# RWKV attention followed by a feed-forward block on one core: a new start-up (small loads issued by GpSimd, r of pair 0 behind k, tables from two banks) and a new order

## The chip, the cores and the metric

The kernel runs on one core of one Trainium2 chip. Its engines work beside each other, each through a queue of its own in the order written: TensorE (PE, matmuls), VectorE (DVE), ScalarE (ACT), GpSimd (POOL) and SyncE (SP, which here only issues transfers). They wait for each other through semaphores. The metric is the device time of the whole program in microseconds (us), median of the runs.

## What is computed

The reference, cut to what matters (B = 4, H = 8 heads, S = 768 steps, D = 48; the result of the first part, seen as 4 x 768 x 384, is the input of the second):

```python
state = 0
for t in range(S):                                   # for every batch and head
    cur = outer(u * k[t], v[t])
    y[t] = r[t] @ (state + cur)
    state = w[:, None] * state + outer(k[t], v[t])
# second part, x = y with the heads side by side (C = 384)
mu = mean(x); var = mean((x - mu) ** 2)
xn = (x - mu) / sqrt(var + 1e-6) * g_ln
out = x + maximum(xn @ w_ch1, 0) @ w_ch2             # 384 -> 1536 -> 384
```

## The kernel before, in words

The 4 x 768 steps are 24 tiles of 128 steps, six to a batch. Within a tile the recurrence is done as masked attention: k is multiplied by powers w^-(t+1) and r by powers w^t (the tables Fk and Fr), both are transposed on PE or by a transposing transfer, `AT` multiplies them into scores, `AM` masks them on DVE, `S` makes the tile's state (and the column sums for the u term), `ZU` scales the state with the decay, `Y` adds the state's and the scores' parts, `X` adds the u term. The second part of each tile: `SQ` and `RS` for the norm, `XN` centres, `LT` and `XT` (or `LTD`) transpose, `UP` is the first product (12 matmuls a step), `RL` the relu out of PSUM, `DN` the second product, `OT` the sum, `STO` the store.

The first four tiles are two pairs. A pair is loaded in one transfer for each of k, r and v (`LK2`, `LR2`, `LV2`, 384 KB each), and its steps have a 2 in their names: `SK2` and `SR2` multiply by the tables `Fk2` and `Fr2`, `TRk2` and `TRr2` transpose into PSUM, `TCk2` and `TCr2` copy that to SBUF, `Q2` multiplies the two transposed tensors, `AT2`, `AM2`, `CC2`, `VB2`, `Y2` as above. For pair 0 k is done by halves of the heads (`SKH`, `TRH`).

The tables come from w: `WF` loads w as a row, `LN` takes its logarithm into `ln_row` (whose other rows `MO` sets to 0, and `ones` to 1), `WBM` spreads the row over the 128 partitions with a matmul by ones, and `FK2`, `FR2`, `FK`, `FR` are ACT exponentials of that with a power of each partition (`MI2` makes `pow2` and `MI` makes `pow_i` and the identity on GpSimd). `ROWS` loads w, u and g_ln as 11 rows; `RM` turns them into columns on PE, `RC` copies them out; `UW`, `WL`, `UGC` make from them the u term's factors, the decay of a tile (WLZ) and -g. `SW` folds -g into the first weights (`LW1` loads them), `IW2` loads the second weights with a cast through GpSimd. `MP`, `MZ`, `MM`, `MM2`, `MR` are memsets and masks. `DU,n` is n columns of dummy matmuls on zeros.

All steps stand in one list, PLAN, written out. An entry is step, number and engine (`v` DVE, `s` ACT, `g` GpSimd, `-` the engine that the step always has; for a transfer the letter names the queue: `-` SP, `s` ACT). The entries are issued in this order, so each engine's queue is the list cut to its steps; nothing is moved later. The waits follow from the tiles' users. Buffers are rings (SLOTS; four of `ot`, so OT of tile i + 4 waits for the store of tile i); in PSUM two banks serve `hp`, and `at` (two banks wide), `s`, `y`, `tr` and `o` have one buffer each. In the program's transfers eight semaphores take turns, so that a transfer from SP or ACT waits for the one eight before it.

Lines that matter: L225 and L223 issue the rows, L304 is LN, L314 WBM, L321 the tables, L203 every product of two tensors, L200 and L198 every copy, L299 and L301 the dummies, L532 the pair transposes, L431 and L580 AT, L448 and L590 AM, L461 to L476 S of a pair, L715 UP, L743 DN, L799 OT, L809 the stores.

Of the kernel before, what the change touches and what calls it, by code (L numbers as in the profile page):

```python
# [29 lines left out]
UP,33,- RL,32,s LK,7,- RS,1,s Y,4,- RL,33,s UP,34,- XT,3,s DN,5,- SQ,2,s TRr2,3,- RL,34,s UP,48,- RS,2,s TCr2,3,v SK,5,g DN,6,- LR2,4,- MP,6,g UP,49,-  # L30
OT,1,v VB,4,g LV,6,- TRk,5,- DN,0,- TCk,5,v SK,6,v DN,1,- LK,8,- RL,48,s ZU,4,v TRk,6,- Q,5,v DN,2,- TCk,6,s SK,7,v AT,5,- LK,11,- OT,0,v Q,6,g
UP,50,- X,4,v LK,9,- TRk,7,- AM,5,v SR2,4,g DN,8,- XN,4,s SQ,3,s DN,9,- LV,7,- TCk,7,v CV,5,s S,5,- DN,10,- RL,49,v RL,50,s SK,8,g LR2,5,- LT,4,-
CC,5,s AT,6,- OT,2,v XT,4,s Y,5,- VB,5,g AM,6,v SQ,4,s LK,10,- UP,64,- CV,6,s SK,11,g UP,65,- SK,9,v RL,64,s LR2,6,- TRr2,4,- X,5,v S,6,- TCr2,4,s
DN,12,- Q,7,v TDk,4,- XN,5,g ZU,6,v Y,6,- DN,13,- SR2,5,v CV,7,g RL,65,s LT,5,- LV,8,- RS,3,s AT,7,- SK,10,v DN,14,- XT,5,s RS,4,s UP,66,- CC,6,s
STO,0,- OT,3,v VB,6,g LV,9,- UP,80,- AM,7,v RL,66,s SR2,6,g TRr2,5,- SQ,5,s TDk,5,- S,7,- X,6,v TCr2,5,s DN,16,- ZU,7,v AT,9,- Q,8,v UP,81,- RL,80,s
LK,13,- ZD,7,v CC,7,v AM,9,v Y,7,- VB,7,g TRr2,6,- STO,3,- DN,17,- CV,8,g STO,1,- TCr2,6,s XN,6,v LK,12,- DN,18,- X,7,v UP,82,- STO,2,- CV,9,s OT,4,v
RL,81,s LV,10,- S,8,- Q,10,v AT,8,- RL,82,s ZU,8,v DN,20,- RS,5,s Q,9,v ZD,8,g CC,8,s AM,8,v XN,7,s DN,21,- LK,15,- LT,6,- S,9,- XT,6,s DN,22,-
ZU,9,v SQ,6,s LV,13,- UP,96,- VB,8,v CC,9,v OT,5,v LT,7,- VB,9,g Y,9,- RL,96,s UP,98,- STO,5,- XT,7,s ZD,9,g X,9,v LV,11,- AT,10,- CV,10,v UP,97,-
LK,14,- XN,9,g SK,12,v Y,8,- SK,13,g RL,97,s DN,24,- AM,10,v RL,98,s LV,12,- DN,25,- RS,6,s Q,11,g SQ,7,s X,8,v LT,9,- S,10,- TDk,6,- UP,112,- CC,10,v
XN,8,v VB,10,g DN,26,- RL,112,s LR2,7,- UP,113,- SQ,9,s SK,15,g OT,6,v LK,16,- Y,10,- ZU,10,v RL,113,s UP,114,- XT,9,v ZD,10,g X,10,v LT,8,- AT,11,- RL,114,s  # L40
LV,15,- DN,28,- SK,14,g XT,8,s AM,11,v CV,12,s S,11,- UP,130,- CV,11,g LK,17,- UP,131,- RL,130,v Y,11,- LV,14,- Q,12,v RL,131,s UP,129,- CC,11,s XN,10,s VB,11,g
AT,13,- LR,17,- RL,129,s DN,29,- SR2,7,g CV,13,s X,11,v UP,128,- AM,13,v XN,11,s S,12,- RS,7,s UP,133,- LTD,9,- SQ,8,s ZU,12,v Q,13,g DN,30,- RL,128,v SQ,10,s
TRr2,7,- STO,4,- OT,7,v RL,133,s CV,15,g UP,132,- LR,16,- SQ,11,s SK,17,g AT,12,- TDk,7,- RL,132,v TCr2,7,s DN,32,- CV,14,g SK,16,v DN,33,- LR,19,- CC,12,s RS,8,s
AM,12,v VB,12,g DN,34,- S,13,- LV,16,- SR,17,g UP,149,- OT,8,v CC,13,s UP,147,- VB,13,g RL,149,s LK,19,- Y,13,- RL,147,v SR,16,g DN,36,- X,13,v STO,6,- UP,145,-
Q,14,g ZU,13,v TDr,8,- Y,12,- UP,146,- RL,145,v XN,13,g Q,15,v DN,37,- RL,146,s X,12,v AT,14,- DN,38,- XN,12,s AM,14,v UP,144,- LTD,10,- OT,9,v UP,148,- RL,144,s
ZD,13,v S,14,- RS,9,s TDk,8,- DN,40,- SK,19,v RL,148,s ZU,14,v AT,15,- SQ,12,s Y,14,- LK,18,- AM,15,v CC,14,s DN,41,- VB,14,g STO,7,- S,15,- LR,18,- DN,42,-
X,14,v CV,16,v UP,163,- XN,14,s ZD,14,v LV,18,- UP,165,- OT,10,v RL,163,s Q,16,v Y,15,- RL,165,s ZU,15,v UP,161,- LV,19,- CC,15,s SQ,13,s VB,15,g UP,160,- RL,161,s
LV,17,- AT,17,- X,15,v RS,10,s DN,44,- RL,160,s AM,17,v XN,15,g DN,45,- ZD,15,g CV,18,s LTD,11,- DN,46,- SK,18,v SR,19,g UP,164,- OT,11,v STO,8,- UP,162,- TDk,9,-
RL,164,s Q,17,g AT,16,- RL,162,s DN,48,- AM,16,v LK,21,- SR,18,g DN,49,- S,16,- UP,177,- TDr,9,- CC,16,v ZU,16,v DN,50,- RL,177,s ZD,16,v UP,176,- VB,16,v STO,9,-
OT,12,v LR,20,- Y,16,- RL,176,s S,17,- STO,10,- UP,181,- X,16,v CC,17,s LK,20,- VB,17,g UP,178,- RL,181,s CV,17,g DN,52,- SQ,14,s LR,21,- Q,19,g Y,17,- SQ,15,s  # L50
DN,53,- X,17,v XN,16,s DN,54,- RL,178,s RS,11,s UP,180,- OT,13,v XN,17,s AT,18,- Q,18,v RL,180,s UP,179,- LTD,12,- AM,18,v SK,20,g CV,19,s DN,56,- RL,179,s SK,21,v
LV,20,- S,18,- DN,57,- ZU,18,v CC,18,s STO,11,- SQ,17,s VB,18,g Y,18,- STO,12,- AT,19,- DN,58,- TDk,10,- SR,20,g AM,19,v UP,197,- SR,21,g X,18,v UP,195,- RL,197,s
OT,14,v S,19,- TDr,10,- SQ,16,s UP,193,- RL,195,v CC,19,s CV,20,s Y,19,- ZU,19,v XN,18,s DN,60,- LV,21,- VB,19,v ZD,19,g DN,61,- X,19,v RL,193,v UP,192,- XN,19,s
SQ,19,s DN,62,- LTD,13,- RL,192,v RS,12,s UP,194,- OT,15,v SQ,18,s UP,196,- Q,21,v LV,22,- RL,194,s Q,20,v AT,20,- LR,23,- RL,196,s DN,64,- AM,20,v RS,13,s DN,65,-
CV,21,s LR,22,- S,20,- DN,66,- LK,23,- ZU,20,v UP,211,- ZD,20,g OT,16,v LK,22,- AT,21,- CC,20,v RL,211,s UP,213,- SR,23,g AM,21,v STO,13,- S,21,- UP,208,- STO,14,-
CC,21,s RL,213,s ZU,21,v VB,21,g Y,21,- SR,22,v RL,208,s DN,68,- X,21,v DN,69,- TDr,11,- VB,20,v XN,21,g DN,70,- UP,209,- SK,23,g OT,17,v LTD,15,- Y,20,- SK,22,v
RL,209,s UP,210,- CV,22,s X,20,v TDk,11,- UP,212,- RL,210,s DN,72,- SQ,20,s RL,212,v DN,73,- XN,20,s SQ,21,s DN,74,- LTD,14,- UP,242,- OT,18,v UP,241,- LV,23,- ZD,21,v
# [55 lines left out]

# [738 lines left out]
```

## Time and profile before

| | before |
|---|---|
| median of 3 runs | 148.47 us (148.46 to 148.66) |
| profiled execution | 147.94 us |
| its span, first to last instruction | 146.2 us |
| PE busy | 140.7 us (96%) |
| DVE, ACT, POOL busy | 108.5, 88.7, 76.8 us |
| transfers | 27.24 MB, 186 GB/s over the span |
| dummy columns in PLAN | 12880 |
| first AT2 of pair 0 starts | 10.53 us |
| first UP starts | 20.32 us |

A row of the timeline gives start, duration, engine, line, operation, the tiles by name (buffer numbers left out), the number of instructions merged, and in brackets the idle time before with what ended it. `SPq`, `ACTq`, `POOLq` are the issuing of a transfer; the transfer itself goes on after that. A tile's name is that of its buffer: `sc<-kf,Fk` is SK or SKH, `sc<-rf,Fr` is SR, `trs<-tr` is TC, `A<-at,mask` is AM. In a stretch table the columns are the stretch, the sum of busy time (with number of instructions) of PE, weight loads, DVE, ACT and POOL, the granted clock of PE, the share of the transfer engines, and GB/s.

### The profile page before, as it was taken

Reading aid. Unit: us, or ns where it says so; the run is one execution under the profiler, and the core shown is the slowest. Engines: PE = TensorE matmul, PEld = TensorE weight load, DVE = VectorE, ACT = ScalarE, POOL = GpSimd, SP = SyncE. Lnnn points to the kernel's source line nnn. Section 1 sums busy time; section 2 is a strip of 40 time slices with the busy share of each in tenths; the row PEclk is TensorE's granted clock in tenths of the full one; section 3 lists DMA queues with packets and bytes.
Section 4 is the critical chain, followed back from the end, with each engine's and each line's share of the span. In section 5 each row is a group of like instructions: output and inputs, shape, how many; then the busy total and the mean of one; then the engine's idle time right before and its main releaser. Section 6 shows DMA issues by size and latency. Waiting matters only on the chain.

```text
span 146.2 us, 4682 instructions
## 1 busy us (share of the span) xinstructions
PE 140.7 (96%) x1909; PEld 110.3 (75%) x1909; DVE 108.5 (74%) x207; ACT 88.7 (61%) x211; POOL 76.8 (53%) x107
## 2 busy tenths in 40 slices
PE   6899999999999999999999999999999999998990
...
GB/s 114 246 322 393 350 238 227 212 239 170 248 69 188 96 305 213 193 220 168 166 204 186 126 211 149 215 229 148 222 104 207 262 114 100 108 31 172 106 86 99
DMA packets 86021, 27.24 MB, mean 186 GB/s; under 512 B 81260, under 2 KB 84464, under 8 KB 86000
## 3 DMA queue, kind: packets, MB, share of 16 engines
...
q0 software_dynamic: 432, 1.18, 4.5%
q10 hardware_dynamic: 2086, 0.79, 2.1%
...
q14 instruction: 6, 0.05, 0.1%
HBM read 18.88 MB, written 4.72 MB: 161 GB/s over the span
## 4 chain that ended last, share of the span: by engine, by line
PE 86%; DVE 4%; POOL 3%; DMA 1%; SPq 1%; issue 1%; ACT 1%; POOLq 0%; ACTq 0%; DVEq 0%
PE hp L715 32%; PE o L743 30%; PE at L580 5%; PE y L652 3%; PE tr L532 2%; PE s L615 2%; PE y L644 2%; PE o L299 2%; DVE sc L203 1%; DMA out_dram<-ot 1%; PE y L511 1%; PE tr L700 1%; PE s L602 1%; SPq L809 1%; PE s L476 1%
## 5 line engine op out<-in xcount | busy, mean ns | idle before, releaser
L715 PE MATMUL hp<-xT,w_sb 128*128 128x128 bf16 (+1 forms) x648 | 57.0, 237 | 0.0
L731 ACT ACTIVATE hT<-hp 128x512 bf16<-128x512 f32 x58 | 34.1, 594 | 32.7 <-PE hp L715 29.5
L743 PE MATMUL o<-w_sb,hT 128*128 128x384 bf16 x276 | 52.9, 326 | 0.4 <-DVE ot L799 0.4
L715 PEld LDWEIGHTS <-w_sb 128*128 128x128 bf16 x648 | 49.0, 114 | 3.7 <-DMA xT<-xn 0.2
L743 PEld LDWEIGHTS <-hT 128*128 128x128 bf16 x276 | 24.4, 97 | 13.3 <-issue 0.5
L590 DVE TENSOR_TENSOR A<-at,mask 128x1024 bf16<-128x1024 f32 x20 | 24.4, 1220 | 2.8 <-PE at L580 2.8
L634 POOL TENSOR_TENSOR Vb<-vf,cc 128x384 f32<-128x384 f32 x15 | 13.2, 879 | 20.5 <-ACT cc L198 13.4
L799 DVE SCALAR_TENSOR_TENSOR ot<-o,rs,x 128x384 f32<-128x384 f32 x23 | 14.2, 616 | 9.1 <-PE o L743 5.9
L659 DVE SCALAR_TENSOR_TENSOR x<-y,Vb 128x384 f32<-128x384 f32 x24 | 13.2, 551 | 8.0 <-POOL Vb L634 4.4
L203 POOL TENSOR_TENSOR q<-trs,trs 128x512 bf16<-128x512 bf16 x9 | 10.5, 1170 | 10.5 <-ACT trs L198 5.9
L203 POOL TENSOR_TENSOR sc<-rf,Fr 128x384 bf16<-128x384 f32 (+1 forms) x11 | 14.6, 1331 | 1.7 <-DMA rf<-in_r_dram 1.6
L666 ACT ACTIVATE sqj<-x,sm 128x384 bf16<-128x384 f32 x24 | 14.6, 609 | 0.1
L198 ACT COPY trs<-tr 128x1024 bf16<-128x1024 bf16 (+1 forms) x10 | 10.8, 1075 | 4.0 <-PE tr L532 3.6
L203 DVE TENSOR_TENSOR sc<-kf,Fk 128x384 bf16<-128x384 f32 (+1 forms) x14 | 10.3, 739 | 3.0 <-ACT Fk L321 2.9
L733 DVE TENSOR_SCALAR hT<-hp 128x512 bf16<-128x512 f32 x14 | 9.6, 688 | 3.9 <-PE hp L715 3.8
L203 POOL TENSOR_TENSOR Z<-ZS,WLZ 128x384 bf16<-128x384 f32 x7 | 7.3, 1045 | 9.8 <-DVE ZS L628 9.8
L673 ACT ACTIVATE xn<-x,sm 128x384 bf16<-128x384 f32 x14 | 8.6, 612 | 4.3 <-DVE x L659 4.2
L203 POOL TENSOR_TENSOR sc<-kf,Fk 128x384 bf16<-128x384 f32 x9 | 9.0, 1000 | 3.0 <-DMA kf<-in_k_dram 3.0
L299 PE MATMUL o<-warm 128*128 128x512 bf16 x21 | 7.1, 463 | 1.2 <-DVE warm L250 1.2
L580 PE MATMUL at<-trs,trs 48*128 48x128 bf16 x160 | 7.9, 219 | 0.0
L198 ACT CAST vv<-vf 128x384 bf16<-128x384 f32 (+1 forms) x13 | 6.9, 531 | 1.0 <-DMA vf<-in_v_dram 0.9
L628 DVE TENSOR_TENSOR ZS<-s,Z 128x384 f32<-128x384 f32 x12 | 6.6, 553 | 0.8 <-PE s L615 0.7
...
## 6 DMA issues: line engine op xcount, KB each, us to landing
...
```

Of the source, the lines that this page charges most:

```text
L198: nc.scalar.copy(out=out, in_=in_)
L203: engines[e].tensor_tensor(out=out, in0=in0, in1=in1, op=ALU.mult)
L299: nc.tensor.matmul(out=warm_ps[0][:], lhsT=warm[:, :P], rhs=warm[:], start=True, stop=True)
L580: nc.tensor.matmul(out=t[:, par, q, :], lhsT=kT(i)[p0 : p0 + D, q, :], rhs=rT(i)[p0 : p0 + D, q, :], start=True, stop=True,)
L590: engines[e].tensor_tensor(out=eqt(AA(i)[:]), in0=eqt(src[:]), in1=mask[:].unsqueeze(1).to_broadcast([P, H, P]), op=ALU.mult)
L634: engines[e].tensor_tensor(out=heads(Vb(i)), in0=vf(i), in1=cc(i)[:].unsqueeze(2).to_broadcast([P, H, D]), op=ALU.mult,)
L659: nc.vector.scalar_tensor_tensor(out=xx(i)[:], in0=psum["y", i][:, :C], scalar=1.0, in1=Vb(i), op0=ALU.mult, op1=ALU.add, accum_out=sm[i][:],)
L666: nc.scalar.activation(out=sqj[:], in_=xx(i)[:], func=ACT.Square, bias=sm[i][:], scale=-float(C), accum_out=sq[g][:, j : j + 1])
L715: nc.tensor.matmul(out=t[:, a * gw : (a + 1) * gw], lhsT=w1_sb[n][kc][:, fb::FB], rhs=xT(g)[:, :size, kc, :], start=(kc == 0), stop=(kc == ...
L731: nc.scalar.activation(out=o, in_=s, func=ACT.Relu)
L743: nc.tensor.matmul(out=psum["o", i][:, :C], lhsT=hT(g)[:, fk, j * P : (j + 1) * P], rhs=w2_sb[d][:, a, :], start=(fk == 0), stop=(fk == FK ...
L799: nc.vector.scalar_tensor_tensor(out=ot(i)[:], in0=psum["o", i][:, :C], scalar=rs[g][:, j : j + 1], in1=xx(i)[:], op0=ALU.mult, op1=ALU.add,)
```

## The change

The code adds a queue for GpSimd's transfers and the steps `SRH`, `TRG` and `GQ`; it splits `FK`, `FR` and `FR2` by halves of the heads; and it gives the two halves of WBM two banks (`y` and `hp`) in place of the two banks of `at`. The transposed r of pair 0 goes to an `hp` bank in place of `tr`. The diff, with PLAN cut to its first lines, and then two places near its end:

```diff
-MW,0,v LV2,0,s WF,0,- MZ,0,v MM2,0,g LK2,0,- MO,0,v TL,0,s MP,2,v MR,0,v MP,0,g MI,0,g ROWS,1,- ROWS,0,- MI2,0,g IDF,0,v LN,0,s LR2,0,- MP,7,g ROWS,2,s
-DU,3104,- WBM,0,- MM,0,g LK2,1,- MP,3,g CV2,0,g WBM,1,- FK2,0,s FK2,1,s LR2,1,- FK2,2,s SKH,0,v FK2,3,s DU,1008,- RM,0,- FR2,0,s SKH,1,v DU,176,- TRH,0,- LR2,2,s LV2,1,-
-MP,1,v DU,176,- TRH,1,- MP,5,v FR2,1,s TCk2,0,s SR2,0,v FR,0,s SK2,1,v DU,3008,- TRr2,0,- RC,0,s FK,0,s UW,0,g TCr2,0,v WL,0,s LW1,0,- MP,4,v DU,2304,- AT2,0,-
-Q2,0,v SR2,1,g LW1,1,- AM2,0,v DU,640,- S,0,- LK,4,- TRk2,1,- ZU,0,v AT2,1,- LW1,2,- TCk2,1,s CC2,0,v VB2,0,g AM2,1,v CV2,1,s DU,2048,- TRr2,1,- LV,4,- SR2,2,v
-S,1,- TCr2,1,s Y2,1,- ZU,1,v UGC,0,s Q2,1,v TRr2,2,- SW,0,s SW,2,g AT2,2,- X,1,v S,2,- TCr2,2,s AM2,2,v DU,416,- Y2,0,- LR2,3,- XN,1,s ZU,2,v CC2,1,s
+MW,0,v LK2,0,s WF,0,- MP,0,v MP,3,g MZ,0,v MM2,0,g LR2,0,- TL,0,s MR,0,v MP,2,v MP,1,v MO,0,v ROWS,2,g LK2,1,- LN,0,s MI2,0,g LV2,0,s DU,2592,- WBM,0,-
+ROWS,0,g LR2,1,- WBM,1,- ROWS,1,g FK2,0,s FK2,1,s MI,0,g FR2,1,s SKH,0,v FK2,2,s FK2,3,s IDF,0,g MP,5,v FR2,0,s DU,1648,- TRH,0,- SKH,1,v FR2,2,s LR2,2,- SRH,0,v
+FR2,3,s DU,400,- TRH,1,- RM,0,- SRH,1,v TCk2,0,s SK2,1,v TRG,0,- TRG,1,- LV2,1,- RC,0,s FK,1,s TCr2,0,v UW,0,g UGC,0,s FR,1,s FK,0,s Q2,0,v DU,2256,- AT2,0,-
+LW1,0,- CV2,0,s TRk2,1,- AM2,0,v GQ,0,g WL,0,s LW1,1,- S,0,- SR2,1,g TCk2,1,s LK,4,- ZU,0,v DU,832,- AT2,1,- MP,7,v CC2,0,s LW1,2,- FR,0,s DU,592,- S,1,-
+AM2,1,v SR2,2,g TRr2,1,- ZU,1,v LV,4,- DU,64,- Y2,1,- TCr2,1,s VB2,0,v CV2,1,s DU,688,- TRr2,2,- Q2,1,v AT2,2,- TCr2,2,s X,1,v DU,336,- S,2,- AM2,2,v XN,1,g
+SW,2,s SW,1,g DU,368,- LT,1,- Y2,0,- LR2,3,- SW,0,s CC2,1,v XT,1,v MP,4,v ZU,2,v SW,3,g SW,5,s AT2,3,- SK,4,v UP,16,- IW2,0,g SW,4,s X,0,v TRk,4,-
...
-UP,225,- OT,19,v XN,22,s AT,23,- RS,14,g SQ,22,s UP,226,- LTD,16,- AM,23,v RL,225,s RS,16,g DN,80,- RL,226,s STO,18,- S,23,- Y,23,- CC,23,s STO,16,- DN,81,- VB,23,g
-UP,240,- X,23,v DN,82,- RL,240,s XN,23,g UP,257,- OT,20,v LTD,17,- UP,256,- RL,257,s DN,84,- SQ,23,s RL,256,v STO,17,- UP,258,- STO,20,- RS,17,g DN,85,- RL,258,v RS,15,g
+LTD,15,- Y,20,- SQ,21,s SK,23,v UP,213,- RL,211,s DN,68,- STO,13,- RL,213,v TDk,11,- UP,210,- X,20,v DN,69,- ZU,21,v RL,210,s XN,20,v STO,16,- DN,70,- SQ,20,s LTD,14,-
+UP,225,- LTD,16,- S,23,- UP,242,- OT,19,v CC,23,s RL,225,s Y,23,- VB,23,v RL,242,s DN,80,- X,23,v DN,81,- SQ,23,s DN,82,- XN,23,s RS,17,g UP,257,- OT,20,v LTD,17,-
...
-    queues = {"-": nc.sync, "s": nc.scalar}
+    queues = {"-": nc.sync, "s": nc.scalar, "g": nc.gpsimd}
...
+    told = const.tile([1, 2], BF16, name="told")
...
+    def SRH(h, e):
+        hh = slice(h * HP, (h + 1) * HP)
+        times(e, sc(1)[:, :, hh, :D], slots(rf2(0))[:, :, hh], Fr2[:, :, hh])
+
+    def TRG(h, e):
+        for j in range(2):
+            q0 = j * HP + h * (HP // 2)
+            turn(1, q0, q0 + HP // 2)
+
+    def GQ(i, e):
+        engines[e].tensor_copy(out=told[:], in_=q2[0][0:1, 0, 0, 0:2])
...
     def WBM(i, e):
-        if i == 0:
-            psum["wb"] = ps.tile([P, 2, HP, P], FP32, name="at")
-        half_bank = psum["wb"][:, i].rearrange("p q t -> p (q t)")[:, :CH]
-        nc.tensor.matmul(out=half_bank, lhsT=ones[:], rhs=ln_row[:, i * CH : (i + 1) * CH], start=True, stop=True)
-
-    def table(out, pw, h=None):
-        src = psum["wb"][:].rearrange("p b q t -> p b (q t)")[:, :, :CH]
-        dst = out.rearrange("p (b h) d -> p b (h d)", b=2)
-        if h is not None:
-            src, dst = src[:, h], dst[:, h]
-        nc.scalar.activation(out=dst, in_=src, func=ACT.Exp, scale=pw)
-
-    def FK_(i, e):
-        table(Fk[:], pow_i[:, 1:2])
-
-    def FR_(i, e):
-        table(Fr[:], pow_i[:, 0:1])
-
-    def FR2(j, e):
-        table(Fr2[:, j], pow2[:, j : j + 1])
+        p = psum["wb", i] = (ps_h if i else ps).tile([P, 512], FP32, name="hp" if i else "y")
+        nc.tensor.matmul(out=p[:, :CH], lhsT=ones[:], rhs=ln_row[:, i * CH : (i + 1) * CH], start=True, stop=True)
+
+    def table(out, pw, h):
+        dst = out[:, h * HP : (h + 1) * HP].rearrange("p h d -> p (h d)")
+        nc.scalar.activation(out=dst, in_=psum["wb", h][:, :CH], func=ACT.Exp, scale=pw)
+
+    def FK_(h, e):
+        table(Fk[:], pow_i[:, 1:2], h)
+
+    def FR_(h, e):
+        table(Fr[:], pow_i[:, 0:1], h)
+
+    def FR2(i, e):
+        h, j = divmod(i, 2)
+        table(Fr2[:, j], pow2[:, j : j + 1], h)
...
-            psum["tr", i] = ps.tile([P, 2 * HP, P], BF16, name="tr")
+            psum["tr", i] = ps_h.tile([P, 2 * HP, P], BF16, name="hp") if i == 1 else ps.tile([P, 2 * HP, P], BF16, name="tr")
```

All other lines of PLAN differ too: the same steps in another order and in part on other engines. The dummy columns are 9776 in all, 2592 of them ahead of WBM. For some steps the engine changes: CC of a tile is on DVE 11 times (6 before), SK on GpSimd 13 times (9), SR2 on GpSimd 6 of 7 (4 of 8), RL on DVE 17 of 72 (14).

More of the change, by code (lines that the diff above doesn't have):

```diff
@@ L30 @@
[L30 to L57, printed above, removed]
@@ new lines @@
+XN,3,s Y2,2,- SW,8,v SW,7,g RL,1,v LK,6,- UP,0,- MP,6,g X,2,v IW2,2,g UP,2,- RL,0,s XN,2,v DN,4,- Q,4,g RL,2,s LT,2,- SQ,0,s UP,18,- XT,2,v
+MM,0,g CV,4,v UP,32,- RL,18,v LK,7,- S,4,- RL,32,v LT,3,- UP,34,- XT,3,s AM,4,v UP,33,- RL,34,s DN,5,- SR2,3,v CC,4,s RL,33,s VB,4,g UP,48,- LV,5,-
+TRr2,3,- SK,5,g Y,4,- TCr2,3,s DN,6,- LR2,4,- X,4,v UP,49,- OT,1,v XN,4,g SQ,3,s LV,6,- TRk,5,- SK,6,v DN,0,- TCk,5,s DN,1,- LK,8,- Q,5,v RL,48,s
+ZU,4,v TRk,6,- RS,0,s AT,5,- SK,7,v TCk,6,s DN,2,- LV,8,- RL,49,v SR2,4,g S,5,- LT,4,- OT,0,v UP,50,- CC,5,s LK,9,- XT,4,s AM,5,v RS,3,s DN,8,-
```

37 lines of the change are left out of this document (30 added, 7 removed).

## The prediction

> **What bounds the kernel now.** I read the page's parts 1 and 2 first, then the waits of TensorE, then the timeline of the first 21 us, the stretch table, and the end of the chain.
>
> ```profile
> PE 140.7 (96%) x1909; PEld 110.3 (75%) x1909; DVE 108.5 (74%) x207; ACT 88.7 (61%) x211; POOL 76.8 (53%) x107
> ...
> PE   6899999999999999999999999999999999998990
> ```
>
> TensorE (PE) is busy all along. So the time is three things: when the real work can begin, how many dummy columns (DU) stand in PE's queue, and what stalls the new order brings. The real matmuls are the same before and after.
>
> ```profile
> 1.18 2.74 PE L299 MATMUL o<-warm 128*128 128x512 bf16 x6 [1.18 <-DVE warm L250]
> ...
> 2.40 0.80 SPq L225 DMA_DIRECT2D x<-in_u_dram  x1
> ...
> 2.48 0.52 ACT L304 ACTIVATE ln_row<-x 1x384 f32<-1x384 f32 x1
> ...
> 3.78 1.63 PE L314 MATMUL at<-ln_row,ones 128*128 128x192 f32 x4
> ...
> 3.92 0.44 SPq L394 DMA_DIRECT2D rf<-in_r_dram  x1
> ...
> 5.51 0.42 ACT L321 ACTIVATE Fk<-at,pow 128x192 f32<-128x192 f32 x1 [2.50 <-POOL vv L200]
> ...
> 6.27 1.18 DVE L203 TENSOR_TENSOR sc<-kf,Fk 128x384 bf16<-128x384 f32 x2 [2.91 <-ACT Fk L321]
> ...
> 9.66 0.69 DVE L200 COPY trs<-tr 128x1024 bf16<-128x1024 bf16 x1
> ...
> 10.53 0.42 PE L431 MATMUL at<-trs,trs 48*64 48x128 bf16 x16
> ...
> 20.32 1.53 PE L715 MATMUL hp<-xT,w_sb 128*128 128x128 bf16 x24
> ```
>
> Columns: start, duration, engine, line. The first table (5.51) starts 0.10 after the fourth broadcast matmul ends at 5.41: both halves lie in one tile, so it waits for both. r of pair 0 is issued only at 3.92, behind u and w on SP. The first real score matmul (AT2,0) starts at 10.53, the first UP at 20.32. The dummies end within 0.1 us of what the next real matmul waits for (10.50 against the copy's end at 10.35), so their column counts are close to real waits.
>
> ```profile
> 2.00:4.00 2.00, 2.00 (x7) 0.87 (x6) 0.54 (x4) 0.99 (x2) 1.76 (x12) 1.00 0.99 255
> 4.00:6.00 2.00, 2.00 (x6) 1.19 (x6) 0.00 (x0) 0.49 (x2) 1.44 (x4) 1.00 0.80 183
> 6.00:8.00 2.00, 1.55 (x15) 1.06 (x15) 1.56 (x5) 1.86 (x6) 0.00 (x0) 1.00 1.17 323
> ```
>
> The last column is GB/s: the transfers have a hole at 4 to 6 us, because r was issued late.
>
> ```profile
> 128.59 1.24 DVE A L590
> 129.83 1.41 SPq L809
> 131.30 2.09 DMA out_dram<-ot
> 133.47 0.63 DVE ot L799
> ```
>
> The chain's only late detour: OT,20 waits for the store of tile 16, issued late. PE's idle time there is 0.37. Between 20 us and there I find no PE wait above 0.2 us.
>
> **The start, step by step.** I walk the new order with durations of these rows; "before" times stand in brackets.
>
> *Logarithm and tables.* On DVE the memsets are reordered: four that now stand ahead of ln_row's take 0.13 to 0.20 each, so ln_row ends at 2.65 (2.10) and LN runs 2.70 to 3.22 (3.00). Five 512-column dummies at 0.43 and a short one end PE's lead at 3.34 (3.71), so WBM,0 starts at 3.41 (3.78). Its two matmuls end 0.99 later, 4.40; the other half is in another bank, so the first table starts at 4.50, 1.0 earlier. Tables follow 0.31 apart with 0.42 each: FK2,1 ends 5.23, FK2,3 6.14, FR2,0 6.45, FR2,3 7.06. FR2 in halves adds two ACT instructions, inside this pace.
>
> *Loads.* k takes v's place on ACT's queue at 0.72; v landed in 3.4, so k lands at 4.1. r is second on SP at 1.14, where k was (landed 5.3), so r lands at 5.3. k of pair 1 and v follow without the hole: at 323 GB/s, 384 KB take 1.2, so both are in by 7.6.
>
> *Rows on GpSimd.* Three small loads leave SP (0.80, 0.63) and ACT (0.51) and are put into POOL's queue. POOL's three DMA issues in the trace (L369) cost 0.59 to 0.79 each; an ACT or SP issue is 0.4 to 0.8, a POOL memset 0.31. I take 0.6, bounds 0.3 and 0.8. They also move past the memset of sc and the masks (0.3, 1.3). Behind them on POOL wait pow2 (3.7, needed 4.50) and the identity: 0.72 + 0.3 + 1.4 + 3 x 0.6 + 0.5 + 0.75 = 5.5, bounds 4.6 and 6.1. Its user, TRH,0, needs SKH,0 too (5.26 to 5.82), and PE's dummies end about 6.0 to 6.2. So the issues cost nothing; uncovered, they would cost 0.2 each.
>
> *Pair 0.* SKH,1 runs 6.17 to 6.73, SRH,0 6.65 to 7.21, SRH,1 7.13 to 7.69, SK2,1 7.6 to 8.57 (0.96 at 8.74 before), TCr2,0 to 9.2 (0.69). TRH,1 is done at 7.2, so ACT's copy TCk2,0 (1.01) ends at 8.3. PE: TRH, RM, TRG end at 8.0, 2256 dummies at 216 ns per 512 take 0.95. DVE's copy ends last: AT2,0 at 9.3 (10.53), 1.2 earlier.
>
> *The row columns.* RM now stands in PE's queue between TRH,1 and TRG,0 and waits for all three rows; TRG and everything of PE queue behind it. The last row (u) is issued at about 4.4. Hardware-queue rows took 2.6 to 3.2 from issue (u: 2.40 to 5.63); POOL's 384 KB loads took 5.1 at least. RM is free to wait until 7.6 (then TRG 0.45, its drain 0.2, and DVE is ready at 8.5); later than that, each us costs one. I take 3.0, so 7.4, at no cost, because the size is that of the first row; the other end lands at 9.5 and costs 1.9.
>
> For such a load the Trainium skill ("DMA: Bandwidth & Descriptors", section Anatomy of one DMA) gives about 2.0 us fixed plus bytes over bandwidth. By that u would land near 6.4 and RM would not wait; by the trace's 5.1 it would be 9.5. No small load on that queue is in the trace.
>
> *From there to UP,16.* CV2,0 moves from POOL to ACT (0.83). ACT then carries TCk2,0, five short ones, the cast, WLZ (until 11.1), TCk2,1 (until 12.0), and CC2,0 (until 12.1), for which S,1 waits because it reuses the bank: PE is idle some 0.4 there (11.8 to 12.2). Before, PE had 0.29 idle at 16.6. GQ (0.15, nearest the 0.17 of a small copy) makes POOL wait for Q2,0's end at 9.8; behind it are SR2,1 and SR2,2 at 1.81 each, until 13.6. TRr2,1 is reached at 12.9 and TRr2,2 at 14.5, so GQ costs nothing there. Without it POOL would start SR2,1 when r of pair 1 lands, about 8.8, beside Q2: the trace has the same DVE product at 0.96 alone (7.84) and 1.62 beside a POOL product (14.10), so up to 0.7 on the chain to S,0.
>
> The Trainium skill ("SBUF — State Buffer", section Who interferes with whom) says that a two-input VectorE operation and a reading GpSimd operation exclude each other. That agrees with the 1.62, and puts the guard's worth at the full rest of POOL's product; the sum stays.
>
> AT2,1, TRr2,1, Y2,1, AT2,2, S,2, LT,1, Y2,0, AT2,3 then follow on PE with waits under 0.1, and UP,16 starts at 18.1. Its weight slices end at 17.9 (SW,0 on ACT). S,3 and TRk,4, which stood ahead of it, come after: 0.93. So like for like 19.05 against 20.32: 1.25 earlier. This holds 224 fewer dummy columns after AT2,0 (0.1) and the rest from AT2,0.
>
> **The rest of the list.** STO,16 moves far ahead of OT,20, so the 0.37 wait at 133.5 should go: a gain of 0.4. Against it, in four places two AT steps that share the bank stand 1.83 to 1.95 of PE work apart from start to start (AT,8/10, 18/19, 20/21, 22/23; never under 2.7 before). From an AT's start to its mask's end is 1.61 (128.22 to 129.83). That leaves 0.2 to 0.3 if DVE is free; a DVE operation in the way (0.55 to 0.62) makes 0.3 to 0.4 each. Bounds 0 and 1.5; I take 0.4, as DVE is busy three quarters of the time but planned around. Net zero.
>
> Sum: -1.25 - 0.4 + 0.4 = -1.25. The profiled execution is 147.94 with a span of 146.2; its span should become about 144.95. It lies 0.5 under the median of 148.47, to which I apply the same difference: 147.2.
>
> **Rivals.**
> 1. *The rows land late (slower).* Place: RM in PE's queue. Speaks for it: POOL's loads took 5.1 to 7.2. Against: those are 256 times larger. AT2,0 comes 1.65 after the landing (RM, TRG, dummies). Break-even is a landing at about 8.9; with 5.1 it is 9.5 to 9.6, AT2,0 at 11.2, and with ACT's columns late as well the kernel ends 0.6 slower: 149.1.
> 2. *The early gain is lost in the rest.* DVE late at the four AT pairs and elsewhere for 0.7 more than taken: 147.9 (mild). The store wait kept, 1.5 at the pairs and 0.1 or more elsewhere: 148.8 and above (severe, on the slower side too).
> 3. *The gain is cut* because PE runs at half speed longer. Before 6 us 512 columns take 0.43, later 0.22. If that change came 3 us later, TRH, TRG and 400 dummies would take 1.05 more, 0.3 of it free before DVE's copy ends; AT2,0 would be at 10.05 and the result 148.0. Against: PE has no gap until 6 in either order.
>
> The Trainium skill ("TensorE: Matmul & The Clock Gate", Part 1) states that the full clock comes after one busy window of about 3.4 us. The trace agrees: half pace from 1.18 to about 6, then full. By that rule rival 3 needs the window to end in the thinner stretch after 6.2.
>
> **Chances.** Forecast 0.59, rival 2 mild 0.12, rival 3 0.05; rows late by about 1 us (147.9 to 148.7) 0.07; rival 1 in full 0.08, rival 2 severe 0.09, for an order of 120 us that I did not walk. A measurement of this kernel tells about 0.2% (0.3 us) from no change: faster is under 148.17, slower above 148.77. Faster: 0.59 + 0.12 + 0.05 = 0.76. Same: 0.07. Slower: 0.08 + 0.09 = 0.17. The range: low 146.5 (no AT stalls, and 0.3 more from the walk); high 148.7, which leaves out the slower cases.
>
> **What would show it.** First table at 4.5; r landed by 5.4; AT2,0 near 9.3, ended by DVE's copy; UP,16 near 18.1; no wait of OT on a store near 132. Wrong if RM waits past 7.6, if the identity ends after 6.2, or if PE shows waits on DVE's masks (L599 there) that sum above 1 us.

## The result, and the profile after

The changed kernel takes 150.33 us in the median (148.5 to 155.95, 20 executions), the kernel before 148.27 (147.56 to 150.52, 20 executions beside them). The ratio is 1.0109 (95% interval 1.008 to 1.0137): slower by 1.1%, where 147.2 was forecast. Every ratio in this document leaves out executions more than 1.5% above the quickest of the same kernel (here six, above 150.7), while the medians and ranges hold all. The execution that was profiled is one of the quickest: 148.82, span 147.0, against 147.94 and 146.2 before.

The page of the changed kernel, parts 1 and 2:

```profile
PE 139.9 (95%) x1903; PEld 110.5 (75%) x1905; DVE 110.9 (75%) x217; ACT 87.3 (59%) x202; POOL 84.0 (57%) x115
...
PE   6959999999899999999999999999999999999991
```

PE does 0.8 less work (dummies) and the span is 0.8 longer, so 1.6 more stands idle. The 5 in the third slice (7.35 to 11.0) is new. The timeline of the start, in the manner of the rows before (L325 is WBM, L329 the tables, L541 the pair transposes, L236 RM, L440 AT2, L724 UP):

```profile
3.35 0.99 PE L325 MATMUL y<-ln_row,ones 128*128 128x192 f32 x2
...
4.21 0.60 POOL L226 DMA_DIRECT2D x<-in_u_dram  x1
4.44 0.73 ACT L329 ACTIVATE Fk<-y,pow 128x192 f32<-128x192 f32 x2 [1.23 <-PE y L325]
...
5.30 0.61 POOL L272 TENSOR_SCALAR_AFFINE_SELECT ident<-ident 128x128 bf16<-128x128 bf16 x1
...
6.91 0.54 PE L541 MATMUL tr<-ident,sc 128*128 128x128 bf16 x4
...
9.00 0.36 PE L236 MATMUL s<-idf,x 11*128 11x11 f32 x2 [1.56 <-DMA x<-in_u_dram]
...
10.79 0.42 PE L440 MATMUL at<-trs,trs 48*64 48x128 bf16 x16
...
19.39 0.80 PE L724 MATMUL hp<-xT,w_sb 128*128 128x128 bf16 x11
```

The first table starts at 4.44 (5.51 before). k landed at 4.21, r at 5.41. DVE is done with both products of r at 7.63, and PE with k's transposes at 7.45. But PE stands at RM until 9.00, because u's row, issued at 4.21, lands at 8.87. AT2,0 starts at 10.79, later than the 10.53 before. UP,16 starts at 19.39; with the two steps moved behind it (0.93) that is 20.32, the same as before. The chain of waits has it as one long piece (start, duration, what):

```profile
4.21 4.66 DMA x<-in_u_dram
```

The stretch table of the changed kernel has no hole in the transfers at 4 to 6 us (183 GB/s before), and next to no PE in the 1.8 us ahead of RM:

```profile
4.00:6.00 2.00, 2.00 (x7) 1.06 (x6) 0.70 (x2) 1.56 (x6) 1.80 (x7) 1.00 1.17 324
...
7.20:9.00 1.80, 0.24 (x4) 0.10 (x2) 1.30 (x2) 1.01 (x1) 0.00 (x0) 1.00 1.18 321
```

At the other end the chain is PE alone where it went through a store of tile 16 before:

```profile
131.81 1.97 PE o L752 x12
133.78 0.04 issue
133.82 1.53 PE hp L724 x24
```

In between the timeline shows waits that the kernel before did not have:

```profile
34.63 2.10 POOL L204 TENSOR_TENSOR sc<-rf,Fr 128x768 bf16<-128x768 f32 x1
35.08 1.93 DVE L204 TENSOR_TENSOR q<-trs,trs 128x512 bf16<-128x512 bf16 x1
...
37.53 0.24 PE L611 MATMUL s<-uwI,q 128*128 128x2 bf16 x4 [0.22 <-DVE Z L204]
...
39.12 0.81 PE L752 MATMUL o<-w_sb,hT 128*128 128x384 bf16 x4 [0.49 <-DVE ot L808]
```

GpSimd's product of r of pair 4 (SR2,4) runs, and beside it DVE's Q of tile 5 takes 1.93, with Z and OT behind it. From matmul to matmul PE loses 0.23, 0.38 and 0.66 at 34 to 39. These waits and the lost start explain the profiled execution. They do not explain why the median lies 1.5 above it.

### The profile page after: what moved, and what is told of

Its sections match the earlier page's. It is cut to its first block, busy times and chain, and to the rows that moved or that the text cites. A ratio compares the mean times of both kernels' runs of the same rounds, so it can differ in the third digit from the quotient of the medians.

```text
span 147.0 us, 4656 instructions
## 1 busy us (share of the span) xinstructions
PE 139.9 (95%) x1903; PEld 110.5 (75%) x1905; DVE 110.9 (75%) x217; ACT 87.3 (59%) x202; POOL 84.0 (57%) x115
## 4 chain that ended last, share of the span: by engine, by line
PE 85%; DVE 4%; DMA 3%; POOL 3%; issue 1%; ACT 0%; POOLq 0%
PE hp L724 32%; PE o L752 29%; PE at L589 4%; DMA x<-in_u_dram 3%; PE y L661 3%; PE tr L541 2%; PE y L653 2%; PE s L624 2%; PE y L520 2%; DVE q L204 1%; PE s L485 1%; PE tr L709 1%; PE s L611 1%; POOL Vb L643 1%; PE at L440 1%
## 5 line engine op out<-in xcount | busy, mean ns | idle before, releaser
L724 PE MATMUL hp<-xT,w_sb 128*128 128x128 bf16 (+1 forms) x648 | 57.2, 238 | 0.1
L724 PEld LDWEIGHTS <-w_sb 128*128 128x128 bf16 x648 | 49.0, 114 | 4.5 <-DMA xT<-xn 0.4
L740 ACT ACTIVATE hT<-hp 128x512 bf16<-128x512 f32 x55 | 32.2, 596 | 33.1 <-PE hp L724 32.4
L204 POOL TENSOR_TENSOR sc<-rf,Fr 128x768 bf16<-128x768 f32 (+1 forms) x9 | 14.2, 1583 | 0.7 <-DMA rf<-in_r_dram 0.7
L204 POOL TENSOR_TENSOR sc<-kf,Fk 128x384 bf16<-128x384 f32 x13 | 13.7, 1058 | 0.3 <-ACT cc L199 0.3
L742 DVE TENSOR_SCALAR hT<-hp 128x512 bf16<-128x512 f32 x17 | 11.3, 682 | 2.9 <-PE hp L724 2.8
L204 POOL TENSOR_TENSOR Z<-ZS,WLZ 128x384 bf16<-128x384 f32 x9 | 9.2, 1021 | 5.2 <-DVE ZS L637 4.5
L684 POOL TENSOR_SCALAR xn<-x,sm 128x384 bf16<-128x384 f32 x8 | 5.0, 626 | 9.6 <-DVE x L668 9.5
L204 DVE TENSOR_TENSOR sc<-kf,Fk 128x384 bf16<-128x384 f32 (+1 forms) x10 | 6.6, 662 | 2.8 <-ACT Fk L329 2.8
L682 ACT ACTIVATE xn<-x,sm 128x384 bf16<-128x384 f32 x10 | 6.1, 610 | 3.3 <-DVE x L668 3.3
L204 DVE TENSOR_TENSOR q<-trs,trs 128x512 bf16<-128x512 bf16 (+1 forms) x12 | 7.3, 611 | 0.6 <-DMA trs<-sc 0.5
L661 PE MATMUL y<-vv,A 128*128 128x48 bf16 x160 | 7.2, 183 | 0.0
```

Of the source, the lines that this page charges most:

```text
L204: engines[e].tensor_tensor(out=out, in0=in0, in1=in1, op=ALU.mult)
L661: nc.tensor.matmul(out=t[:, h * D : (h + 1) * D], lhsT=AA(i)[:, par, q, :], rhs=vv(i)[:, h, :], start=first, stop=True, skip_group_check=True,
L724: nc.tensor.matmul(out=t[:, a * gw : (a + 1) * gw], lhsT=w1_sb[n][kc][:, fb::FB], rhs=xT(g)[:, :size, kc, :], start=(kc == 0), stop=(kc == ...
L740: nc.scalar.activation(out=o, in_=s, func=ACT.Relu)
```

## The experiments

All are timed against the kernel before, beside which they ran. Only PLAN is edited, unless a line says otherwise. Line numbers differ by a few between the kernels.

### First: the row, the queue, the idle stretch, the order

**rm_late** moves the matmul of the rows and its users behind the last dummies ahead of AT2,0.

```diff
-TRH,1,- RM,0,- SRH,1,v ... TRG,1,- LV2,1,- RC,0,s FK,1,s TCr2,0,v UW,0,g UGC,0,s FR,1,s ... DU,2256,-
+TRH,1,- SRH,1,v ... TRG,1,- LV2,1,- FK,1,s TCr2,0,v FR,1,s ... DU,2256,- RM,0,- RC,0,s UW,0,g UGC,0,s
```

> RM, RC, UW and UGC moved from between TRH,1 and TRG,0 to behind the 2256 dummies; the rows still go through GpSimd and still land near 8.9 us. Theory A (PE stood still for u's landing): no PE wait above 0.3 us before AT2,0, which starts at 9.3 instead of 10.8; profiled span about 145.7 (147.0 - 1.3). Theory B (the idle stretch at 7.2 to 9.0 also costs full clock in most executions): the median falls by more than A's 1.3, to about 147.5 from 150.2, and the mean granted clock is 0.998 or more in nearly all runs. Without B: about 148.9. Rival C (the three issues on POOL are what hurt, by a late identity): no change, AT2,0 stays near 10.8.

Measured: 148.06 us, ratio 1.0017 (0.9985 to 1.005); span 146.1. The timeline of rm_late:

```profile
7.92 1.03 PE L308 MATMUL o<-warm 128*128 128x512 bf16 x4
...
8.97 0.39 PE L232 MATMUL s<-idf,x 11*128 11x11 f32 x2
9.29 0.42 PE L436 MATMUL at<-trs,trs 48*64 48x128 bf16 x16
```

RM no longer waits, AT2,0 starts at 9.29, UP,16 at 18.55, and 2.3 us of the median are gone (the span is 0.4 above theory A's 145.7). So PE's wait for the row is shown to be a cause. The waits at 33 to 38 (0.24, 0.39, 0.66) are still there.

**rows_sp** issues the three rows from SP behind k of pair 1 (`ROWS,2,-` `ROWS,0,-` `ROWS,1,-` after `LK2,1,-`).

> The three row loads issued by SP right behind LK2,1 instead of by GpSimd, all else as in the changed kernel. Theory A: the rows land by about 7, RM runs at 7.3, AT2,0 at 9.3, profiled span about 145.7. Theory B: median about 147.5, clock 0.998 or more. Rival C: better than the run with RM late by the 0.2 to 0.6 that a freer POOL gives; if SP's 2 us of issuing delays r of pair 1 past 11, AT2,0 keeps its gain and TRr2,1 loses some.

Measured: 149.35, ratio 1.0084 (1.0053 to 1.0114). u is issued at 4.94, RM starts at 8.32 and AT2,0 at 10.12, not at 9.3. From SP u lands 3.25 after its issue (4.66 from GpSimd), but it is issued later, behind the large loads. The other two rows took 3.93 and 5.59 by the counts of their semaphores, and all three landed at 7.83 to 8.19. So moving the rows to SP's queue does not mend it.

**fill** puts `DU,2560,-` ahead of RM, so that PE is busy while it waits for the row.

> 2560 dummy columns put ahead of RM (1.07 us at full clock), so that PE is busy while it waits for the rows; nothing else changes. Theory A: AT2,0 still at 10.8, profiled span 147.0 within 0.3. Theory B: the executions with a mean clock of 0.988 and 150 us and more go away: median about 148.7 instead of 150.2. Without B: the median stays at 150.2.

Measured: 149.74, ratio 1.0103 (1.0074 to 1.0131); mean granted clock 0.999 or 1.0 in each of six executions. The time hardly fell, which looks like the end of theory B and is not: its profile has another loss, a wait of 1.35 at 123. In the timeline of fill (L640 is VB, L698 a transposing load, L815 a store, L805 OT):

```profile
115.34 1.00 POOL L201 TENSOR_TENSOR sc<-kf,Fk 128x384 bf16<-128x384 f32 x1
...
115.67 1.09 DVE L640 TENSOR_TENSOR Vb<-vf,cc 128x384 f32<-128x384 f32 x1 [0.87 <-ACT cc L196]
...
117.95 1.19 SPq L698 DMA_TRANSPOSE xT<-xn  x1
...
119.19 0.57 SPq L815 DMA_DIRECT2D out_dram<-ot  x1
...
123.72 0.62 DVE L805 SCALAR_TENSOR_TENSOR ot<-o,rs,x 128x384 f32<-128x384 f32 x1 [2.47 <-DMA out_dram<-ot]
```

and in that of the changed kernel:

```profile
115.70 0.56 DVE L643 TENSOR_TENSOR Vb<-vf,cc 128x384 f32<-128x384 f32 x1 [0.87 <-ACT cc L199]
115.71 1.42 POOL L204 TENSOR_TENSOR sc<-kf,Fk 128x384 bf16<-128x384 f32 x1 [0.29 <-ACT cc L199]
...
118.68 0.57 SPq L818 DMA_DIRECT2D out_dram<-ot  x1
```

In fill the k of tile 22 landed at 115.16 (the last count of its semaphore), before DVE started, so GpSimd's product went first and DVE's VB took 1.09. In the changed kernel's profile it landed at 115.64, DVE went first (0.56) and GpSimd's product took 1.42. DVE's 0.5 then passes through X, XN and SP's queue to the store of tile 13, which lands at 123.61 instead of 120.85. OT of tile 17 writes the same buffer and waits, and PE behind it. Of these 2.76 only 0.51 is the later issue. The rest is a longer way from issue to landing (4.42 against 2.17), and its cause is not shown: in the profile of rows_first VB took 0.56 and this store still took 4.11.

**early_before_rest_after** keeps before's list up to UP,16 and takes the rest in the new order.

> The kernel before up to UP,16 (its start-up unchanged), then the remaining steps in the changed kernel's order on the changed kernel's engines. Theory D (the new order loses 1.4 us of PE time at 34 to 39 us by itself, when a DVE product and a POOL product share their path, Q at 1.93 us): span about 147.2, 1.0 above before. Rival (those stalls come only from the late and changed start): span 145.8 to 146.2, no slower than before.

Measured: 150.24, ratio 1.0132 (1.01 to 1.0163), PE waits of 0.40 at 26.8, 0.26 and 0.66 at 37 to 38, 1.31 at 122.8 (OT, its store) and 0.28 at 134.5. The span of 148.4 is above both forecasts, and 1.31 of the 2.2 lost is the store's wait.

### Second: putting things together, and the store

**rm_late_rest_before** is the opposite graft: rm_late's start, then before's rest.

> The changed kernel's start with the row columns moved behind the dummies (the start of rm_late), and from the first UP on the order of the kernel before, on the engines of before. Theory A+D (the change lost time in two places, TensorE standing still for u's row and the new order past UP,16, and they add): AT2,0 at 9.3, UP,16 at 18.5, no stalls of DVE's Q and OT at 34 to 39; like for like UP,16 is 0.8 to 1.8 earlier than before's 20.32 (two steps, worth 0.93, have moved behind it), so the span is 145.0 to 145.4 against 146.2 and the median about 147.1 (146.7 to 147.5). Rival (the rest gives the early gain back whatever its order is, because later waits are set by loads and stores): median 148.0 to 148.5, as rm_late and before.

Measured: 148.93, ratio 1.0068 (1.0046 to 1.0089). Missed by 1.8. The waits at 36 to 38 are gone, but others come: PE waits 0.91 at 24.1 for X, 0.48 at 34.5 for OT, 0.51 at 93.9 and 0.44 at 124.9 for transposing loads, 0.42 at 135.2 for OT. Both grafts lose, so neither says which order is better: each list fits the start that it was written for, and a start 1 to 2 us earlier or later lets other products of DVE and GpSimd, and other issues of SP, meet.

**store_early** moves `STO,13,-` right behind `STO,12,-`.

> The changed kernel with one store moved: that of tile 13 stands right behind the store of tile 12 in SyncE's queue instead of behind X and XN of tile 21. Theory E (the executions above 149.5 are those in which the load of k for tile 22 lands before DVE starts Vb of tile 21 at about 115.7: GpSimd's product then takes the path first, DVE's Vb takes 1.1 instead of 0.56, the transposing DMA behind X on SyncE and the store of tile 13 are issued 0.5 later, the store lands at 123.6, and OT of tile 17, which writes the same buffer, makes TensorE wait 1.35): the store lands before 118, no OT wait at 122 to 124, median 148.5 to 148.9, no fast execution above 149.4. Rival F (the longer executions come from the clock or from something before 110): median 150.0 to 150.5 as the changed kernel's 150.33.

Measured: 150.15, ratio 1.0146 (1.0122 to 1.017). The wait at 122 is gone, but SP was busy there: a transposing load comes later and PE waits 0.84 at 111. Besides, five of six executions had a mean granted clock under 0.99. Inconclusive on the median.

**rows_first** reorders GpSimd's list: tables' exponents (MI2), the rows with u first, the identity, and the masks (MM2) last.

> The changed kernel with GpSimd's list in another order: the tables of exponents first, then the three row loads (u first, issued near 1.9), the identity, and the masks of the pairs last. RM stays where the change put it. Theory G (a row load of GpSimd lands 4.6 after its issue, whenever that is): u 6.5, w 7.2, g 7.8; RM starts at 7.3 to 7.9, AT2,0 at 9.3 to 9.6, UP,16 at 18.1 to 18.6, so 1.2 to 1.5 earlier than the changed kernel's, median 148.6 to 149.2 with the losses of the rest still in it. Rival H (the rows wait for the loads of k, r and v, which fill the DMA engines until 7.9): the last row lands at 8.2 to 8.9, AT2,0 at 10.1 to 10.8, median 150.

Measured: 148.79, ratio 1.0034 (1.0001 to 1.0066). Issues at 2.13, 2.95, 3.57 landed at 6.70, 7.76, 8.10: 4.53 to 4.81 after issue, as 4.56, 4.62 and 4.66 in the changed kernel, whose u was issued 2.1 later. Theory G's delay holds here, but the last row is too late: RM starts at 8.23 and AT2,0 at 10.03, near rival H's 10.1 to 10.8. Four of the twelve executions, at 150.7 to 151.4, had a mean granted clock of 0.985 to 0.987.

**sr24_dve** is rm_late with SR2,4 moved from GpSimd to DVE, behind OT of tile 0.

> As rm_late, with one product moved: SR2,4 (r of pair 4) from GpSimd, where it runs beside DVE's Q of tile 5, to DVE behind OT of tile 0. Theory D (in the new order DVE's Q takes 1.93 instead of 0.42 to 0.6 because GpSimd's product of 2.10 holds the path; it delays Z, and OT): Q takes at most 0.6, TensorE's waits at 36.2 (0.39) and 37.6 (0.66) are gone, span 145.1 to 145.6 against rm_late's 146.1, if DVE's own 0.95 does not bring a wait of its own near AM,5. Rival I (DVE is simply too full here, whoever makes the product): the 1.05 comes back as a wait on AM,5 or OT, span 146.0 to 146.4.

Measured: 148.38, ratio 1.0023 (0.9996 to 1.005). The timeline of sr24_dve:

```profile
34.25 0.42 DVE L200 TENSOR_TENSOR q<-trs,trs 128x512 bf16<-128x512 bf16 x1
...
37.15 1.35 DVE L200 TENSOR_TENSOR sc<-rf,Fr 128x768 bf16<-128x768 f32 x1
...
39.69 0.40 PE L585 MATMUL at<-trs,trs 48*128 48x128 bf16 x8 [0.93 <-DVE A L595]
```

Q takes 0.42 when GpSimd multiplies nothing beside it, against 1.93. Waits of 1.05 (from matmul to matmul) turn into one of 1.09: the product now stands ahead of the mask AM,5 that PE needs. Just behind that mask DVE is idle for 1.04.

### Third: the two repairs, and the guard

**store_gap** is the changed kernel with `STO,13,-` right ahead of `LTD,15,-`, where SP has 0.77 to spare.

> The changed kernel with one store moved: that of tile 13 stands between the transposing loads of r for pair 11 and of X for tile 21 in SyncE's queue, where SyncE otherwise waits 0.77 for XN of tile 21 (116.68 to 117.45 in the changed kernel's profile); a store's issue there takes 0.57. store_early put it where SyncE was busy, and a transposing load behind it came 0.8 late at 111. Theory E (in the longer executions OT of tile 17 waits for this store at 122 to 123): no wait of OT at 122 to 124, none added, median 148.4 to 148.9. Rival F (the longer executions have another cause): median 150.0 to 150.5.

Measured: 150.47, ratio 1.0119 (1.0076 to 1.0163): as slow as the changed kernel, and with no OT wait at 122. Its three executions at full clock took 148.7 to 149.0, the other nine had a mean granted clock of 0.989 or less. One of those is profiled. The stretch table of store_gap (the clock is third from the end):

```profile
7.20:9.00 1.80, 0.00 (x0) 0.00 (x0) 1.31 (x2) 1.00 (x1) 0.00 (x0) 1.00 1.17 323
9.00:9.82 0.82, 0.67 (x9) 0.67 (x10) 0.00 (x0) 0.27 (x2) 0.02 (x1) 1.00 1.16 322
9.82:13.23 3.41, 3.41 (x33) 1.82 (x31) 1.88 (x3) 2.48 (x8) 1.86 (x4) 0.50 1.09 383
```

PE stood still from 7.15 to 9.15, and from 9.82 it had half the clock for 3.41. In the same stretch the changed kernel's profile has 1.00 and 65 matmuls where there are 33 here. AT2,0 starts at 11.97 and UP,16 at 21.29, 1.9 later than at full clock. So theory B was right. A mean clock under 0.99 occurred in 13 of 20 executions of the changed kernel, in 9 of 12 here and 5 of 6 of store_early; in none of 6 of fill (idle stretch mostly filled) and none of 12 of rm_late (no wait).

The length of the idle stretch does not decide alone. These are PE's waits at RM in the profiles of store_gap, store_early and no_guard (below), in this order:

```profile
9.15 0.36 PE L232 MATMUL s<-idf,x 11*128 11x11 f32 x2 [2.00 <-DMA x<-in_u_dram]
...
9.22 0.36 PE L232 MATMUL s<-idf,x 11*128 11x11 f32 x2 [2.07 <-DMA x<-in_u_dram]
...
9.03 0.56 PE L232 MATMUL s<-idf,x 11*128 11x11 f32 x2 [1.88 <-DMA x<-in_u_dram]
```

store_early, with the longest of the three, kept full clock. In these traces every recorded stretch of full clock, and every stretch of half clock that follows one and ends before the kernel does, is a whole number of windows of 3.41. So the window in which PE stood still can be counted back. The window ahead of the loss held 1.88 of idle time in no_guard, 1.99 in store_gap and 2.65 in rows_pool_before. The clock stayed where the fullest window held 1.55 (changed kernel), 1.54 (rows_sp) or 1.53 (store_early, whose 2.07 a window's edge at 7.69 divides). In these six profiles the limit lies between 1.55 and 1.88 of one window.

**sr24_behind** is sr24_dve with SR2,4 behind AM,5 instead of ahead of it.

> As sr24_dve, with SR2,4 on DVE behind the mask AM of tile 5 instead of ahead of it. In sr24_dve the mask came 1.09 late for that, and DVE stood idle 1.04 right after it (39.6 to 40.68). Theory D (at 33 to 38 the new order loses about 1.0 by one product of GpSimd that holds DVE's path): Q at most 0.6, no wait over 0.3 at 36 to 40, span 144.9 to 145.3 in the undisturbed executions, median 147.0 to 147.9. Rival I (DVE is too full there): another wait of 0.7 to 1.1 by 46, span 145.9 to 146.2, median 148.0 to 148.4.

Measured: 148.03, ratio 0.9997 (0.9967 to 1.0027), the quickest 146.84. No wait at 36 to 40 is left, but the median misses theory D's 147.0 to 147.9; the wait for the store came up in the profiled execution (waits of sr24_behind, 118 to 124 us: who, for what, us in total, times, longest):

```profile
DVE ot L804 <- DMA out_dram<-ot: 2.2, 1, 2.2
...
PE o L748 <- DVE ot L804: 0.9, 1, 0.9
```

**best** is sr24_behind with the store as in store_gap:

```diff
-... LTD,15,- Y,20,- SQ,21,s SK,23,v UP,213,- RL,211,s DN,68,- STO,13,- RL,213,v
+... STO,13,- LTD,15,- Y,20,- SQ,21,s SK,23,v UP,213,- RL,211,s DN,68,- RL,213,v
```

> rm_late, sr24_behind and store_gap together: the row columns behind the dummies, SR2,4 on DVE behind AM of tile 5, the store of tile 13 in SyncE's gap. If the three causes (A the late row, D the path at 33 to 38, E the store at 122) are separate and complete: AT2,0 9.3, no wait above 0.4 after 20 us, span 144.9 to 145.3, median 146.9 (146.6 to 147.4), faster than the kernel before. Rival (something later takes the gain back, as in every order tried so far): median 147.7 to 148.3.

Measured: 146.94 (146.72 to 148.39), ratio 0.9938 (0.9905 to 0.997): 0.6% faster than the kernel before, with a median 0.04 from the forecast. The clock never fell under 0.996. Its page, and the first of its waits at 118 to 124, where neither row of sr24_behind is left:

```profile
span 145.0 us, 4655 instructions
...
PE 139.8 (96%) x1903; PEld 110.4 (76%) x1905; DVE 111.2 (77%) x218; ACT 87.3 (60%) x202; POOL 83.0 (57%) x114
```

```profile
POOL q L200 <- DMA trs<-sc: 6.3, 1, 6.3
ACT hT L736 <- PE hp L720: 1.3, 1, 1.3
```

**no_guard** is the changed kernel without `GQ,0,g`.

> The changed kernel without the small copy that guards q of pair 0. In the changed kernel GpSimd is free at 10.11 and waits for Q2's end at 11.4 before it starts SR2,1. Theory (DVE's Q2 and a product on GpSimd exclude each other): SR2,1 starts near 10.2, Q2 and the mask behind it end 0.5 to 1.2 later, the first score matmuls of S move as much, UP,16 at 19.8 to 20.4 instead of 19.39. Rival (the copy guards nothing that counts): UP,16 within 0.2 of 19.39, median as the changed kernel's.

Measured: 153.93, ratio 1.0266 (1.0206 to 1.0326). All six executions had lost clock windows, so it does not price the guard. In the profile the half clock lasts from 8.72 to 22.37, which is four windows; why it is one window in store_gap and four here, no run shows.

### Fourth: what was open

**fill_gap** joins fill and store_gap.

> The changed kernel with 2560 dummy columns ahead of RM (TensorE busy while it waits for u's row, as in fill) and the store of tile 13 in SyncE's gap (as in store_gap). Theory B+E (the changed kernel's median lies 1.5 above its profiled execution because in most executions the idle stretch of 7.2 to 9.0 costs one clock window of 3.4 at half speed, or OT of tile 17 waits 1.35 for its store): mean clock 0.996 or more in every execution, no OT wait at 122 to 124, median 148.5 to 149.0. Rival F (neither accounts for it): median 149.5 to 150.5.

Measured: 148.73 (148.41 to 149.54), mean clock 0.997 or more in all 12, ratio 1.0054 (1.0033 to 1.0075). Together the two repairs account for the 1.6 between the changed kernel's median and this. Neither repair did it alone.

**fill_gap_no_guard** takes `GQ,0,g` out of that.

> As fill_gap, without the small copy that guards q of pair 0. Theory (Q2 on DVE and SR2,1 on GpSimd exclude each other): SR2,1 starts near 10.2, Q2 takes 1.3 to 1.4 instead of 0.69, S,0 and UP,16 come 0.6 to 1.0 later, median 149.1 to 149.9. Rival (the guard is worth nothing at full clock, and no_guard was slow by its clock alone): within 0.2 of fill_gap.

Measured: 150.3, ratio 1.0142 (1.0105 to 1.018), clock 0.998 or more throughout. In its timeline:

```profile
10.50 4.03 POOL L200 TENSOR_TENSOR sc<-rf,Fr 128x768 bf16<-128x768 f32 x2
11.06 1.80 DVE L200 TENSOR_TENSOR q<-trs,trs 128x1024 bf16<-128x1024 bf16 x1
```

Q2 takes 1.80 instead of 0.69. The guard is worth 1.6 in the median here, twice what was expected. (The profiled executions differ by 2.0 in span, but of that 0.4 is u's row, which landed later in this one: RM at 9.32 against 8.90.)

**rows_pool_before** does one part alone: the kernel before, with the rows on GpSimd's queue behind MI2.

```diff
-    queues = {"-": nc.sync, "s": nc.scalar}
+    queues = {"-": nc.sync, "s": nc.scalar, "g": nc.gpsimd}
-MI,0,g ROWS,1,- ROWS,0,- MI2,0,g IDF,0,v LN,0,s LR2,0,- MP,7,g ROWS,2,s DU,3104,-
+MI,0,g MI2,0,g ROWS,2,g ROWS,0,g ROWS,1,g IDF,0,v LN,0,s LR2,0,- MP,7,g DU,3104,-
```

> The kernel before with one part of the change alone: the three row loads leave SyncE and ScalarE for GpSimd's queue, behind the tables of exponents. Theory A (a row on GpSimd's queue lands 4.6 after its issue, and RM holds up TensorE's queue): issues 3.6 to 5.4, last row lands at 9.0 to 9.6, RM there instead of 6.06, AT2,0 3.0 to 3.4 later than 10.53, median 151.0 to 151.8, and in executions in which the idle stretch also costs a clock window 152.5 to 153.5. Rival (r of pair 0, which is now issued 1.3 to 1.9 earlier, makes up for part of it): AT2,0 at 12.0 to 12.8, median 149.5 to 150.5.

Measured: 151.41, ratio 1.025 (1.0202 to 1.0298). Issues at 3.54, 4.31, 4.96 landed at 7.20, 8.10, 9.01 (3.65 to 4.04 after issue, less than the 4.6 taken), and RM waited from 6.06 to 9.14. The profiled execution also had half clock from 8.29 to 15.12, which puts AT2,0 at 15.68, past both forecasts of it. The median is within theory A's, partly by luck: that range was for executions at full clock, and five of the six had a mean clock of 0.977 to 0.989.

## Why the prediction was wrong, step by step

**Right.** *Logarithm and tables*: first table 4.44 (4.50 forecast). *Loads*: k 4.21, r 5.41, v 7.87 (4.1, 5.3, 7.6). *Rows on GpSimd*, the issues: 0.75, 0.67, 0.60 (0.6 each), identity done at 5.91 (5.5, needed by 6.0 to 6.2). *Pair 0*: rm_late, without the late row, has AT2,0 at 9.29 (9.3). There DVE's copy ended at 9.10 (9.2), though RM, in its new place, ended last. *From there to UP,16*: 8.60 in the changed kernel (8.8); PE's wait behind ACT, forecast as 0.4 near 12, is 0.32 at 12.2 in rm_late and does not appear in the later start of the changed kernel. The store wait near 133 is gone.

**The step that failed: "The row columns".** I had it that RM may wait until 7.6, then took 3.0 from issue to landing "because the size is that of the first row", so 7.4. It was 4.66, landing at 8.87. All 42 row loads that the fourteen profiled kernels issue on this queue took 3.65 to 4.97, above the value taken. The size was no guide. Nor is it the queue alone: from SP and ACT the same rows took 2.6 to 3.2 in the kernel before, which has the hole in its transfers, and from SP 3.25 to 5.59 in rows_sp, which has not. How much of the 4.66 is GpSimd's queue and how much the large loads beside it, the runs do not separate. The Trainium skill ("DMA: Bandwidth & Descriptors", Anatomy of one DMA) gives about 2.0 us fixed, by which u was estimated to land at 6.4; the runs on this queue disagree, by a factor of 1.8 to 2.5, while the other transfers run at about 320 GB/s. What came is the case "rows late by about 1 us" (0.07): the landing at 8.87 is 1.27 past the 7.6 that was free, which by the prediction's own rate makes 148.5. Rival 1 in full was a landing at 9.5 and 149.1.

**Missing from that step: the price of standing still.** I priced a late row at one us per us. PE's standing still costs more in most executions (13 of 20), since the clock falls to half for one or more windows of 3.41, each of which is 1.7 us of work. Rival 3 had half the clock, but as a change that comes late, not as a relapse after an idle stretch. The Trainium skill ("TensorE: Matmul & The Clock Gate", Part 1) says that the window runs freely, which agrees with executions of one kernel that differ, and that the clock falls after at least one idle window of about 3.4 us. Here a window that was idle for 1.88 of its 3.41 was enough (no_guard), while 1.55 did not cost the clock in the profiled execution of the changed kernel. What decides between these two figures stays open.

**Mis-sized: "The rest of the list", net zero.** The store gain of 0.4 came. Of the AT pairs nothing shows. In their place DVE and GpSimd met at 34 to 39, for 1.3 us (0.23, 0.38, 0.66). For rm_late the sum closes: UP,16 is 0.84 earlier like for like (18.55 + 0.93 against 20.32), the waits cost 1.29, and before's 0.53 at 133.6 from matmul to matmul is saved: -0.08, and the span fell from 146.2 to 146.1. This is rival 2 between its mild and its severe form, by another mechanism than its AT pairs. Then the store of tile 13, which I did not look at: it moved next to its user, and costs 1.35 in the profile of fill.

**Too small: the guard.** "Up to 0.7 on the chain" was 1.6. The rule that I cited beside it (the Trainium skill, "SBUF — State Buffer", Who interferes with whom: a two-input VectorE operation and a reading GpSimd operation exclude each other) agrees with 0.69 against 1.80 for Q2, 0.42 against 1.93 for Q of tile 5, and 0.56 against 1.09 for VB. I used it at one place and did not search the rest of the list for it.

**The sum of it.** The span is 2.1 above the forecast of 144.95: UP,16 is 1.29 late (19.39, not 18.1), the waits at 34 to 39 are 0.87 above the 0.4 taken, and the store at the end saves 0.13 more. The other 1.0 of the median lies in the clock and the store of tile 13: it is 1.5 above the profiled execution, where 0.5 was applied.

**Also off**: UP,16 in rm_late at 18.55, not 18.1. best has a span of 145.0, as forecast, with the row out of PE's way, one product moved and one store earlier. That agreement is luck in part: of its 1.2 the start gives 0.84 (1.25 forecast) and the rest 0.37 (nothing forecast).
